# Turning one tile's keys on TensorE instead of VectorE, in a fused window-attention and feed-forward kernel

## The chip, the cores and the metric

The kernel runs on one core of a Trainium2 chip. The metric is the device time of one execution in microseconds (us). Beside it stands a profile of one execution: for each engine (TensorE or PE, its weight loads or PEld, VectorE or DVE, ScalarE or ACT, GpSimd or POOL, SyncE or SP) the instructions in order of time, what ended each wait, and the packets of the DMA queues.

## What is computed

A sliding-window causal attention (window of 64, 8 batches, 8 heads, 576 positions, head size 64), whose output is laid out as 4608 tokens of 512, goes through a gated feed-forward block:

```python
scores = scale * np.matmul(q, k.transpose(0, 1, 3, 2))
rel = pos[:, None] - pos[None, :]
mask = (rel >= 0) & (rel < window)
scores = np.where(mask, scores, -1000000000.0)
attn = softmax(scores)                      # exp, divided by the sum
x = np.matmul(attn, v)                      # then (tokens, heads * head size)
g = x @ w_gate
silu = g * (1.0 / (1.0 + np.exp(-g)))
out = silu * (x @ w_val) @ w_out            # 512 -> 1536 -> 512
```

Inputs and output are fp32; the kernel computes in bf16 with fp32 accumulation.

## The kernel before, in words

**Tiles.** The 4608 tokens are nine tiles of 512. Tile t below 7 holds the first 512 positions of batch t; tile 7 (`LAST`) gathers the last 64 positions of all batches; tile 8 is batch 7. For each tile TensorE computes scores, sums of the exponentials, the mix with the values, then twelve gate steps `m` (`gate_value`, L441: four matmuls with `w_gate` and four with `w_val`, each of 128x128 weights and 512 columns; `gate_end`: ScalarE's silu at L434, VectorE's product `hT` at L435), and later the projection with `w_out` (`project_part`, L450). Tile t's attention is run between the pieces of tile t-1's projection.

**Engines are in order.** The program is written out by hand under a manual schedule: each engine does its instructions in the order of the code. A DMA is an instruction of the engine whose queue it is put on: GpSimd issues most loads (they cast fp32 to bf16 on the way), and a copy that waits on GpSimd holds back the loads behind it.

**Memory for results.** PSUM has eight banks. Banks 0 to 3 are two tiles `two` of two banks each; banks 4 to 7 are four tiles `one`. Gate steps use banks 4 to 7 in turn, except steps 0 and 1 of tile 0, which use the `pairs` of banks (2, 3) and (0, 6).

**Tile 0** is loaded in fp32 (`raw`, `v_first`), cast (`cast_first`, L556), turned by transposes on TensorE (`turn_first`, `transposes`, L207) and copied out of PSUM by VectorE or ScalarE (`split_k`, L210, reorders the keys). Its values: the first half, `v_first`, comes fp32 over SyncE's queue and is cast into `v1` by VectorE (L633, L635); the second half comes cast over GpSimd's queue.

**Tiles 1 to 8** have their queries and keys turned by VectorE, which transposes 32x32 blocks (`turn_q`, L219, and `turn_k`, L229). For that the second 32 of the 64 head dimensions must lie in other partitions than the first. From tile 2 on the load itself arranges this (`load_q`, `load_k`, four DMAs for each part, L91 and L138). For tile 1 it is done in two steps: `load_plain` (L112, L118) brings both halves together, eight key loads and four query loads on GpSimd's queue, and `second_halves` (L130) copies the second half across partitions, one copy on GpSimd and one on ScalarE for each of keys and queries and each half of the heads (`lo`, `hi`).

**The order on GpSimd's queue in the first 50 us** is: two casts for tile 0, half of its values, ten loads of `w_gate` and `w_val` up to column 1024, tile 1's keys `lo`, weights to 1280, queries `lo`, the copy of the keys `lo`, weights to 1536, keys `hi`, the copy of the queries `lo`, `w_out` rows of chunks 0 and 1 (L199), queries `hi`, the copy of the keys `hi`, the rest of `w_out`, three loads of tile 1's values (L164), the copy of the queries `hi`, five more; then all of tile 2.

**Tile 1's turns** lie in tile 0's gate steps: keys after steps 6, 7, 10 and 11, queries after 8 and 9 and, for `hi`, behind step 11. Then come `scores(1, 0)` (L281), sixteen projection matmuls of tile 0 over four banks (`columns(0, 4)`), `scores(1, 1)`, twelve more, the sums (L314), twelve, the mix (L381), and eight. **Tile 2's turns** (`turn`, a query and a key turn for each head pair) lie behind steps 4, 6, 8 and 10 of tile 1's gates; later tiles' behind 1, 4, 7 and 10.

Of the kernel before, what the change touches and what calls it, by code (L numbers as in the profile page):

```python
# [8 lines left out]
P = 128  # L9
FP32 = mybir.dt.float32  # L10
BF16 = mybir.dt.bfloat16
# [6 lines left out]
def kernel(  # L18
# [10 lines left out]
    nc = tc.nc  # L29
    S, D, H = 576, 64, 8  # L30
# [7 lines left out]
    stage = ctx.enter_context(tc.tile_pool(name="stage", bufs=2))  # L38
# [7 lines left out]
    bank = [two[i][:, j] for i in range(2) for j in range(2)]  # L46
# [5 lines left out]
    kT = [cst.tile([P, 4, 512], BF16, name=f"kT{i}") for i in range(3)]  # L52
    v12 = cst.tile([P, 2, 4, H, D], BF16, name="v12")
    v1 = v12[:, 0]
# [3 lines left out]
    identb = cst.tile([P, P], BF16, name="identb")  # L58
# [6 lines left out]
    def batch(t):  # L65
        return t if t < LAST else t - 1
# [7 lines left out]
    staged, queries, weights, inverse, xT, hT = {}, {}, {}, {}, {}, {}  # L74

    def load_runs(eng, dst, src, t, hs):
        eng.dma_start(  # L77
            dst.rearrange("r h e d -> r h (e d)"),
            src[batch(t), hs, 0:512].rearrange("h (r e) d -> r h (e d)", e=4),
        )  # L80
# [21 lines left out]
                    )  # L102
        return q_s

    def load_plain(t, which, us):

        q_s, k_s = staged[t]
        for a in range(2):
            hs = slice(a + 2 * us.start, a + 2 * us.stop - 1, 2)
            r = slice(64 * a, 64 * a + 32)  # L110
            if which == "q":
                nc.gpsimd.dma_start(  # L112
                    q_s[r, us],
                    q[batch(t), hs, 0:512].rearrange("u (r e) d -> r u (e d)", e=16),
                )
            else:
                for u in range(us.start, us.stop):
                    nc.gpsimd.dma_start(  # L118
                        k_s[r, :, u],
                        k[batch(t), 2 * u + a, 0:512].rearrange("(g r e) d -> r g (e d)", g=4, e=4),  # L120
                    )

    def second_halves(t, which, us, a, copy):

        src, dst = slice(64 * a, 64 * a + 32), slice(64 * a + 32, 64 * a + 64)
        if which == "q":
            ap = staged[t][0][:, us].rearrange("r u (e d) -> r (u e) d", d=D)
        else:
            ap = staged[t][1][:, :, us].rearrange("r g u (e d) -> r g (u e) d", d=D)
        copy(ap[dst][..., 0:32], ap[src][..., 32:64])  # L130

    def load_k(k_s, groups):

# [26 lines left out]
    def load_halves(eng, dst, t, hds=range(H)):  # L160

        for hd in hds:
            w, x, h = hd // 4, hd // 2 % 2, hd % 2
            eng.dma_start(  # L164
                dst[64 * x:64 * x + 64, :, w, h],
                v[batch(t), hd, 0:512].rearrange("(j r) d -> r j d", r=64),
            )
# [23 lines left out]
    def weights_gv(f0, f1, c0=0, c1=4):  # L191
        for src, dst in ((moe_w_gate, wg), (moe_w_val, wv)):
            nc.gpsimd.dma_start(  # L193
                dst[:, c0:c1, f0:f1],
                src[P * c0:P * c1, f0:f1].rearrange("(c r) f -> r c f", r=P),
            )

    def weights_o(c0, c1):
        nc.gpsimd.dma_start(  # L199
            wo[:, c0:c1, :],  # L200
            moe_w_out[P * c0:P * c1].rearrange("(c r) f -> r c f", r=P),
        )
# [6 lines left out]
    def split_k(dst, tp):  # L209
        nc.vector.tensor_copy(  # L210
            dst.rearrange("p (r e) -> p r e", e=4),
            tp.rearrange("p (e r) -> p r e", e=4),
        )

    def turn_q(t, u):

        if u == 0:
            queries[t] = att.tile([P, 4, 512], BF16, name="qT", tag="qT")
        nc.vector.transpose(  # L219
            queries[t][:, u, :].rearrange("r (e x) -> r e x", e=16),  # L220
            staged[t][0][:, u].rearrange("r (e d) -> r e d", d=D)[:, :, 0:32],
        )
# [5 lines left out]
    def turn_k(dst, k_s, u):  # L228
        nc.vector.transpose(  # L229
            dst[:, u, :].rearrange("r (g x e) -> r g e x", g=4, e=4),  # L230
            k_s[:, :, u].rearrange("r g (e d) -> r g e d", d=D)[:, :, :, 0:32],
        )
# [28 lines left out]
    def half(x):  # L261
        return slice(64 * x, 64 * x + 64)
# [215 lines left out]
    def out_tile():  # L478
        return bank[4 + take("g")]
# [27 lines left out]
    v_first = stage.tile([P, 4, H, D], FP32, name="v_f", tag="v", bufs=1)  # L507
    for u in range(4):
        hs = slice(2 * u, 2 * u + 2)
# [43 lines left out]
    on_v, on_p, on_a = nc.vector.tensor_copy, nc.gpsimd.tensor_copy, nc.scalar.copy  # L553

    def cast_first(copy, u, i):
        copy(  # L556
            first[:, i, u].rearrange("r e (h d) -> r h e d", h=2),
            raw[i][:, 2 * u:2 * u + 2],
        )
# [8 lines left out]
    def weigh_first(u):  # L568
        E = eb[u][:, 1:17].rearrange("r (h y) z -> r h (y z)", h=2)
        nc.scalar.activation(E, two[u % 2][:], AF.Exp, scale=0.125)  # L570
        weights[0, u] = E
# [17 lines left out]
    cast_first(on_a, 2, 0)  # L589
    cast_first(on_p, 3, 0)  # L590
    weights_gv(0, 256, 0, 2)
    weights_gv(0, 256, 2, 4)
    weights_gv(256, 512)
    weights_gv(512, 768)
    weights_gv(768, 1024)
    q_s = stage.tile([P, 4, 16 * D], BF16, name="q_s", tag="q")
    k_s = stage.tile([P, 4, 4, 4 * D], BF16, name="k_s", tag="k")
    staged[1] = q_s, k_s
    lo, hi = slice(0, 2), slice(2, 4)
    load_plain(1, "k", lo)  # L600
    weights_gv(1024, 1280)
    load_plain(1, "q", lo)
    second_halves(1, "k", lo, 1, on_p)
    weights_gv(1280, 1536)
    load_plain(1, "k", hi)
    second_halves(1, "q", lo, 1, on_p)
    weights_o(0, 2)
    load_plain(1, "q", hi)
    second_halves(1, "k", hi, 1, on_p)
    weights_o(2, 4)  # L610
    weights_o(4, 8)
    weights_o(8, 12)
    load_halves(nc.gpsimd, vb[1], 1, range(3))
    second_halves(1, "q", hi, 1, on_p)
    load_halves(nc.gpsimd, vb[1], 1, range(3, H))

    cast_first(on_v, 2, 1)
# [12 lines left out]
    scores_first(2)  # L630
    log1()
    weigh_first(2)
    on_v(v1[:, 0], v_first[:, 0])  # L633
    turn_first(3, (4, 5))
    on_v(v1[:, 1], v_first[:, 1])  # L635
    bias_first(3)
    scores_first(3)
    weigh_first(3)
# [13 lines left out]
    log3()  # L652
    inv3()
    part_first((3,), (5,), 0, odd)
    pairs = [(bank[2], bank[3]), (bank[0], bank[6])]
    scale(0, 0, bank[0])
    scale(0, 1, bank[1])
    gate_part(0, (0, 1), pairs, 0)
# [9 lines left out]
    for m in range(12):  # L668
        if m < 2:
            gate_end(0, m, pairs[m])  # L670
        else:
            gate_value(0, m)
        if m == 2:
            for x in range(2):
                for c in range(2):
                    nc.vector.tensor_copy(
                        mask[half(x), 0, c],
                        tri[half(x), x ^ c].rearrange("r (y e) -> r e y", e=16),
                    )
            for i in (1, 2, 4):  # L680
                nc.vector.tensor_copy(mask[:, i:2 * i], mask[:, 0:i])
            for E in eb:
                nc.vector.memset(E[:, 0], 0.0)
        if m in (5, 7, 9):
            which, us = {5: ("k", lo), 7: ("q", lo), 9: ("k", hi)}[m]
            second_halves(1, which, us, 0, on_a)
        if m in (6, 7, 10, 11):
            turn_k(kT[1], staged[1][1], {6: 0, 7: 1, 10: 2, 11: 3}[m])
        if m in (8, 9):
            turn_q(1, m - 8)  # L690

    set_exp()
    second_halves(1, "q", hi, 0, on_a)
    for u in (2, 3):
        turn_q(1, u)
    tiles = [out_tile(), d_tile(), out_tile(), d_tile()]
# [18 lines left out]
    for t in range(1, NT):  # L715
        if t > 1:
            set_exp()
            scores(t, 0)
            project(t - 1, 0)
            if t == 2:  # L720
                stage_v(3)
            o_ps = out_tile()
            project_part(t - 1, (1,), (o_ps,), range(5))
            scores(t, 1)
            sums(t, 0)
            project_part(t - 1, (1,), (o_ps,), range(5, 12))
            project_end(t - 1, 1, o_ps)
            project(t - 1, 2)
            sums(t, 1)
            mix_all(t)  # L730
            project(t - 1, 3)
        set_silu()
        if t + 1 == LAST:
            load_last_v()
        elif t + 1 < NT and t > 1:
            cast_v(t + 1)
        if t + 2 < NT:
            load_qk(t + 2)
            if t > 1 and t + 2 != LAST:
                stage_v(t + 2)  # L740
        if t == 2:
            k_l = load_k(
                cast.tile([P, 4, 4, 4 * D], BF16, name="k_l", tag="c0"),
                [(b, S - P) for b in range(4, 8)],
            )
        turns = (4, 6, 8, 10) if t == 1 else (1, 4, 7, 10)
        for m in range(12):
            gate_value(t, m)
            if m in turns and t + 1 < NT:
                turn(t + 1, turns.index(m))  # L750
            if m == 8 and 3 <= t < 7:
                turn_k(kT[2], k_l, t - 3)
# [32 lines left out]
```

## Time and profile before

| what | us |
|---|---|
| median of 3 runs | 327.34 (327.29 to 328.5) |
| the profiled execution | 328.81 |
| its span, first to last instruction | 327.1 |
| TensorE busy | 315.2 |
| VectorE busy | 219.8 |
| ScalarE busy | 168.9 |
| GpSimd busy, DMA issues counted | 152.0 |
| granted TensorE clock, mean | 0.999 |

Two further rows of the profile matter for reading what follows. The page's slices show the share of busy time of an engine in 40 equal parts of the span, 8.2 us each, in tenths:

```profile
PE   7899889979999999999999999999999999999996
...
DMA  7999899999979999979940999799501300021003
```

TensorE is below nine tenths in the first slices, in the sixth (41 to 49 us) and the ninth (65 to 74 us). The chain of work that ended last, followed back from the end, is TensorE from 68 us on, apart from one passage through ScalarE near 143 us; before that it is mostly loads on GpSimd's queue.

A timeline line gives start, length, engine, line, what it writes and reads with the shapes, and in brackets the idle time before it with what ended it. Matmuls are pipelined, so each one's own length overlaps the next; the distance between starts is the cost of one in a stream.

### The profile page before, as it was taken

How to read it: one execution, taken by the hardware profiler on the slowest of the kernel's cores; microseconds unless marked ns; L12 is line 12 of the kernel's file. 1: busy time of each engine (PE TensorE's matmuls, PEld its weight loads, DVE VectorE, ACT ScalarE, POOL GpSimd, SP SyncE). 2: the span in 40 equal slices, each digit the busy share in tenths (PEclk: the TensorE clock that was granted, in tenths of full speed). 3: DMA queues.
4: the chain of work that ended last, by engine and by line, in shares of the span. 5: the costliest groups of instructions: out<-in, count | busy, mean ns of one | idle time of the engine just before them, and what ended most of it. 6: DMA issues, size and time to landing. Idle time of an engine off the chain costs nothing.

```text
span 327.1 us, 6971 instructions
## 1 busy us (share of the span) xinstructions
PE 315.2 (96%) x2708; PEld 150.4 (46%) x2750; DVE 219.8 (67%) x345; ACT 168.9 (52%) x240; POOL 152.0 (46%) x269
## 2 busy tenths in 40 slices
PE   7899889979999999999999999999999999999996
PEld 4544434434444444445444544445445544444443
DVE  4666665397857776787668766976787666774322
ACT  5855847326833583357535653475337633683310
POOL 5958765896276569556523999464110000000000
PEclk9999999999999999999999999999999999999999
DMA  7999899999979999979940999799501300021003
GB/s 253 200 195 173 127 175 180 193 106 158 184 145 204 154 161 151 199 80 179 224 94 12 145 193 101 48 176 199 124 3 28 89 16 2 2 87 43 2 16 113
DMA packets 83618, 40.36 MB, mean 123 GB/s; under 512 B 64256, under 2 KB 78848, under 8 KB 83584
## 3 DMA queue, kind: packets, MB, share of 16 engines
q0 software_dynamic: 51584, 22.59, 58.4%
q1 hardware_dynamic: 31456, 16.79, 20.9%
q10 hardware_dynamic: 544, 0.52, 0.5%
q8 instruction: 21, 0.34, 0.5%
q14 instruction: 13, 0.11, 0.1%
HBM read 53.02 MB, written 9.44 MB: 191 GB/s over the span
## 4 chain that ended last, share of the span: by engine, by line
PE 77%; DMA 15%; POOL 4%; issue 2%; ACT 1%; DVE 1%; SPq 1%; POOLq 0%; DVEq 0%
PE one L441 46%; PE one L450 24%; DMA k_s<-in_k_dram 6%; DMA wo<-in_moe_w_out_dram 3%; DMA q_s<-in_q_dram 3%; PE two L281 2%; DMA wv<-in_moe_w_val_dram 2%; PE two L381 2%; DMA q_f<-in_q_dram 2%; PE one L314 1%; POOL wg L193 1%; PE one L492 1%; POOL wv L193 1%; POOL k_s L130 1%; SPq L77 1%
## 5 line engine op out<-in xcount | busy, mean ns | idle before, releaser
L434 ACT ACTIVATE sg<-one 128x512 f32<-128x512 f32 x106 | 63.3, 597 | 111.5 <-PE one L441 88.8
L435 DVE TENSOR_TENSOR hT<-sg,one 128x512 bf16<-128x512 f32 x107 | 74.1, 693 | 57.0 <-PE one L441 54.9
L441 PE MATMUL one<-xT,wg 128*128 128x512 bf16 x416 | 108.4, 379 | 0.8
L441 PE MATMUL one<-xT,wv 128*128 128x512 bf16 x414 | 107.0, 379 | 1.9 <-DVE hT L435 1.8
L450 PE MATMUL one<-wo,hT 128*128 128x512 bf16 x397 | 93.9, 380 | 2.8 <-DMA wo<-in_moe_w_out_dram 1.0
L138 POOL DMA_DIRECT2D k_s<-in_k_dram x112 | 60.5, 552 | 27.0 <-DMA q_s<-in_q_dram 18.2
L441 PEld LDWEIGHTS <-wv 128*128 128x128 bf16 x424 | 41.5, 98 | 52.0 <-issue 2.1
L441 PEld LDWEIGHTS <-wg 128*128 128x128 bf16 x424 | 41.5, 98 | 50.2 <-issue 0.3
L450 PEld LDWEIGHTS <-hT 128*128 128x128 bf16 x420 | 39.1, 98 | 48.3 <-issue 3.7
L229 DVE STREAM_TRANSPOSE kT<-k_s 128x512 bf16<-128x512 bf16 x32 | 41.3, 1290 | 2.8 <-DMA k_s<-in_k_dram 2.8
L294 ACT ACTIVATE eb<-two 128x960 bf16<-128x960 f32 (+1 forms) x32 | 29.5, 974 | 16.8 <-PE two L281 16.7
L297 DVE TENSOR_TENSOR eb<-eb,mask 128x960 bf16<-128x960 bf16 (+1 forms) x32 | 21.4, 667 | 12.1 <-ACT eb L294 12.1
L397 DVE TENSOR_TENSOR xT<-two,r 128x512 bf16<-128x512 f32 x34 | 21.7, 686 | 6.4 <-PE two L381 4.8
L189 POOL CAST vb<-v_f 128x512 bf16<-128x512 f32 x20 | 11.4, 616 | 31.3 <-PE one L441 11.6
L219 DVE STREAM_TRANSPOSE qT<-q_s 128x512 bf16<-128x512 bf16 x32 | 22.4, 702 | 1.7 <-POOL q_s L130 1.7
L331 ACT ACTIVATE r<-r 128x512 f32<-128x512 f32 (+1 forms) x34 | 22.3, 655 | 1.0
L328 ACT ACTIVATE r<-one 128x512 f32<-128x512 f32 x32 | 18.9, 590 | 4.8 <-PE one L314 4.7
L91 POOL DMA_DIRECT2D q_s<-in_q_dram x24 | 13.0, 565 | 5.1 <-DVE qT L219 4.8
L302 DVE TENSOR_TENSOR both<-eb 128x512 bf16<-128x512 bf16 x32 | 13.6, 425 | 1.1
L500 ACT ACT_TABLE_LOAD x9 | 11.5, 1283 | 2.0 <-issue 1.9
L164 POOL DMA_DIRECT2D vb<-in_v_dram x16 | 11.0, 734 | 2.6 <-DMA wo<-in_moe_w_out_dram 2.6
L503 ACT ACT_TABLE_LOAD x9 | 11.5, 1283 | 0.2
(115 smaller groups left out, 193.4 us busy)
## 6 DMA issues: line engine op xcount, KB each, us to landing
k_s<-in_k_dram POOLq DMA_DIRECT2D x112, 56.0 KB, 5.2
q_s<-in_q_dram POOLq DMA_DIRECT2D x24, 248.0 KB, 5.4
v_f<-in_v_dram SPq DMA_DIRECT2D x40, 128.0 KB
wg<-in_moe_w_gate_dram POOLq DMA_DIRECT2D x5, 256.0 KB, 6.5
wv<-in_moe_w_val_dram POOLq DMA_DIRECT2D x5, 256.0 KB, 7.2
q_f<-in_q_dram SPq DMA_DIRECT2D x4, 256.0 KB
wo<-in_moe_w_out_dram POOLq DMA_DIRECT2D x2, 512.0 KB, 7.1
vb<-in_v_dram POOLq DMA_DIRECT2D x16, 64.0 KB, 4.2
```

Of the source, the lines that this page charges most:

```text
L138: nc.gpsimd.dma_start(k_s[p0:p0 + 32, g, :, 0:w], k[b, a:H:2, s:s + P].rearrange("u (r e) d -> r u (e d)", e=4) [:, :, 32 * c:32 * c + w],)
L219: nc.vector.transpose(queries[t][:, u, :].rearrange("r (e x) -> r e x", e=16), staged[t][0][:, u].rearrange("r (e d) -> r e d", d=D)[:, :, ...
L229: nc.vector.transpose(dst[:, u, :].rearrange("r (g x e) -> r g e x", g=4, e=4), k_s[:, :, u].rearrange("r g (e d) -> r g e d", d=D)[:, :, ...
L294: nc.scalar.activation(flat, s_ps[h][:].rearrange("r a b -> r (a b)")[:, 0:n], AF.Exp, scale=0.125)
L297: nc.vector.tensor_mul(flat, flat, mask[:].rearrange("r j c e y -> r (j c e y)")[:, 0:n])
L328: nc.scalar.activation(r, d_ps, AF.Ln)
L331: nc.scalar.activation(r, r, AF.Exp, scale=-1.0)
L397: nc.vector.tensor_mul(x, o_ps, r)
L434: nc.scalar.activation(sg[:], g_ps[:], AF.Silu)
L435: nc.vector.tensor_mul(hT[t][:, m, :], sg[:], v_ps[:])
L441: nc.tensor.matmul(ps[:], w[:, c, P * m:P * m + P], xT[t][:, c, :], start=(c == 0), stop=(c == 3),)
L450: nc.tensor.matmul(o_ps[:], hT[t][:, c, P * s:P * s + P], wo[:, c, :], start=(c == 0), stop=(c == 11),)
```

## The change

Tile 1's keys are loaded as they lie, positions in partitions, by two loads of four heads each (`raw_k`, as tile 0's `load_runs` does but cast on the way), and not copied across partitions. After gate steps 6 and 8 TensorE transposes them, for each of two head pairs eight times 128x64 into 64x128 (four position phases, two heads) into bank `u` of 0 to 3, and VectorE copies each bank out with `split_k`, as for tile 0. The eight key loads, the four key copies and VectorE's four key turns of tile 1 are gone.

GpSimd's copies of query halves stand later in its order, behind more loads; ScalarE's copy of the `lo` queries moves from step 7 to 8, and its copy of the `hi` queries goes to VectorE. Tile 1's query turns `lo` move from steps 8 and 9 to 9 and 10. The two casts of `v_first` go from VectorE to GpSimd, between its second and third weight load. The banks of `pairs[1]` are swapped: gate in bank 6, value in bank 0. Tile 2's turns move from steps 4, 6, 8, 10 to 6, 8, 10, 11.

```diff
-    def load_plain(t, which, us):
-
-        q_s, k_s = staged[t]
+    def load_plain(t, us):
+
         for a in range(2):
...
+            nc.gpsimd.dma_start(
+                staged[t][0][64 * a:64 * a + 32, us],
+                q[batch(t), a + 2 * us.start:2 * us.stop:2, 0:512]
+                .rearrange("u (r e) d -> r u (e d)", e=16),
+            )
...
     weights_gv(0, 256, 0, 2)
+    on_p(v1[:, 0], v_first[:, 0])
+    on_p(v1[:, 1], v_first[:, 1])
     weights_gv(0, 256, 2, 4)
...
-    k_s = stage.tile([P, 4, 4, 4 * D], BF16, name="k_s", tag="k")
-    staged[1] = q_s, k_s
+    raw_k = stage.tile([P, H, 4, D], BF16, name="k_r", tag="k")
+    staged[1] = q_s, None
     lo, hi = slice(0, 2), slice(2, 4)
-    load_plain(1, "k", lo)
+    load_runs(nc.gpsimd, raw_k[:, 0:4], k, 1, slice(0, 4))
     weights_gv(1024, 1280)
-    load_plain(1, "q", lo)
-    second_halves(1, "k", lo, 1, on_p)
+    load_runs(nc.gpsimd, raw_k[:, 4:8], k, 1, slice(4, 8))
+    load_plain(1, lo)
     weights_gv(1280, 1536)
-    load_plain(1, "k", hi)
-    second_halves(1, "q", lo, 1, on_p)
     weights_o(0, 2)
-    load_plain(1, "q", hi)
-    second_halves(1, "k", hi, 1, on_p)
+    second_halves(1, lo, 1, on_p)
+    load_plain(1, hi)
     weights_o(2, 4)
     weights_o(4, 8)
     weights_o(8, 12)
     load_halves(nc.gpsimd, vb[1], 1, range(3))
-    second_halves(1, "q", hi, 1, on_p)
+    second_halves(1, hi, 1, on_p)
     load_halves(nc.gpsimd, vb[1], 1, range(3, H))
...
-    on_v(v1[:, 0], v_first[:, 0])
     turn_first(3, (4, 5))
-    on_v(v1[:, 1], v_first[:, 1])
...
-    pairs = [(bank[2], bank[3]), (bank[0], bank[6])]
+    pairs = [(bank[2], bank[3]), (bank[6], bank[0])]
...
-        if m in (5, 7, 9):
-            which, us = {5: ("k", lo), 7: ("q", lo), 9: ("k", hi)}[m]
-            second_halves(1, which, us, 0, on_a)
-        if m in (6, 7, 10, 11):
-            turn_k(kT[1], staged[1][1], {6: 0, 7: 1, 10: 2, 11: 3}[m])
-        if m in (8, 9):
-            turn_q(1, m - 8)
+        if m == 8:
+            second_halves(1, lo, 0, on_a)
+        if m in (6, 8):
+            for u in (m - 6, m - 5):
+                tp = bank[u].bitcast(BF16)[:, 0:512]
+                for e in range(4):
+                    for h in range(2):
+                        nc.tensor.transpose(
+                            tp[half(h), P * e:P * e + P], raw_k[:, 2 * u + h, e], identb[:]
+                        )
+                split_k(kT[1][:, u, :], tp)
+        if m in (9, 10):
+            turn_q(1, m - 9)
 
     set_exp()
-    second_halves(1, "q", hi, 0, on_a)
+    second_halves(1, hi, 0, on_v)
...
-        turns = (4, 6, 8, 10) if t == 1 else (1, 4, 7, 10)
+        turns = (6, 8, 10, 11) if t == 1 else (1, 4, 7, 10)
```

## The prediction

> **What bounds the kernel now.** I read the page's first part, then TensorE's waits, then the timelines of TensorE, VectorE and GpSimd up to 80 us. TensorE is busy 96% of the span, so the time is its work plus its waits.
>
> ```profile
> PE 315.2 (96%) x2708; PEld 150.4 (46%) x2750; DVE 219.8 (67%) x345; ACT 168.9 (52%) x240; POOL 152.0 (46%) x269
> ```
>
> Its waits in total (us, times, longest), without the first 16 us:
>
> ```profile
> PE one L441 <- DVE hT L435: 1.8, 1, 1.8
> ...
> PE one L450 <- DMA wo<-in_moe_w_out_dram: 1.0, 2, 0.5
> ...
> PE one L450 <- DVE hT L435: 0.4, 1, 0.4
> PE two L281 <- DVE qT L219: 0.4, 1, 0.4
> ```
>
> They lie in two places: the stretch where tile 0 is projected while tile 1's scores run (37 to 53 us), and one step of tile 1's gates. In TensorE's timeline (start, length, line, last the idle time and its releaser):
>
> ```profile
> 11.12 0.62 PE L207 MATMUL one<-identb,qk_b 128*128 128x128 bf16 x8
> ...
> 13.81 0.46 PE L360 MATMUL two<-eb,v 128*64 128x64 bf16 x16
> ...
> 16.25 0.38 PE L421 MATMUL two<-xT,wg 128*128 128x512 bf16 x1 [0.22 <-DVE xT L397]
> ...
> 37.07 0.62 PE L281 MATMUL two<-qT,kT 64*64 64x128 bf16 x32
> 37.62 0.82 PE L450 MATMUL one<-wo,hT 128*128 128x512 bf16 x3
> 38.85 1.24 PE L450 MATMUL one<-wo,hT 128*128 128x512 bf16 x5 [0.41 <-DVE hT L435]
> 40.58 1.89 PE L450 MATMUL one<-wo,hT 128*128 128x512 bf16 x8 [0.49 <-DMA wo<-in_moe_w_out_dram]
> ...
> 68.05 1.02 PE L441 MATMUL one<-xT,wv 128*128 128x512 bf16 x4 [1.83 <-DVE hT L435]
> ```
>
> Four 512-column matmuls start 0.864 us after the four before them, so one costs 0.216 us; a gate step (one m) is eight, 1.73 us. VectorE in the same time:
>
> ```profile
> 11.90 0.68 DVE L210 COPY kT<-one 128x512 bf16<-128x512 bf16 x1
> ...
> 14.90 1.29 DVE L397 TENSOR_TENSOR xT<-two,r 128x512 bf16<-128x512 f32 x2 [0.64 <-PE one L360]
> ...
> 28.61 0.69 DVE L435 TENSOR_TENSOR hT<-sg,one 128x512 bf16<-128x512 f32 x1 [1.04 <-PE one L441]
> 29.22 1.32 DVE L229 STREAM_TRANSPOSE kT<-k_s 128x512 bf16<-128x512 bf16 x1
> ...
> 66.16 1.32 DVE L229 STREAM_TRANSPOSE kT<-k_s 128x512 bf16<-128x512 bf16 x1 [2.83 <-DMA k_s<-in_k_dram]
> ```
>
> At 66.16 VectorE has stood 2.83 us for tile 2's keys; the hT behind it is late and TensorE stands. GpSimd, which issues the loads, does the same to itself earlier: it waits for keys before a copy, and the wo loads stand behind.
>
> ```profile
> 35.41 1.03 POOL L130 COPY k_s<-k_s 32x1024 bf16<-32x1024 bf16 x1 [1.84 <-DMA k_s<-in_k_dram]
> 36.39 2.22 POOL L199 DMA_DIRECT2D wo<-in_moe_w_out_dram x3
> ```
>
> The windows view has 196 GB/s from 13 to 27 us, but 110 GB/s from 37 to 42.
>
> **The change, part by part**, on the profiled clock.
>
> *Swap of the second gate pair's banks.* At 16.25 a matmul into bank[0] waits for VectorE. bank[0]'s own reader, the first of the two xT products begun at 14.90, is done at 15.5; the second, which reads bank[1], ends at 14.90 + 1.29 = 16.19. So both halves of a tile `two` are guarded as one. With bank[6] first, that matmul goes ahead: -0.17 (0 to -0.22).
>
> *Two casts of v1 on GpSimd* (0.61 to 0.88 us each by its own L556 casts) stand between its second and third weight load at 10.6 us: the loads behind are issued 1.2 to 1.8 later. The values were issued by SyncE at 4.5 and 4.9 and their packets end by 10.8, so no wait. The cover is the queue: values and first weights are in it until about 13.7. The tightest load is wv 256:512, issued at 12.71 and landed at 19.19 in the chain, read at 20.57: 1.2 us of slack after the swap. I take 0; if nothing is hidden, up to +0.6. VectorE gains nothing: qT at 11.56 follows the end of its transposes anyhow.
>
> *Keys by two loads.* The same bytes. An issue on GpSimd follows the landing of the load eight places earlier (the chain: a load issued at 12.71 lands at 19.19, the eighth after it goes out at 19.47); two loads for eight leave more bytes in flight, and no key copy stops GpSimd. The first four heads landed at 26.00; now about 26.4, needed by TensorE at 28.2. The second load, about two weight loads of 1.35 and its own 1.3 later, at 30.4, is needed at 33.5. Both hidden; beyond those margins each us late is one lost. The query copy that GpSimd still waits for (q landed about 31.5) now has wo 0:2 and the last weights issued ahead of it. Those weights landed at 33.9 against 34.4 before; the later gates only widen that. No cost.
>
> *Transposes on TensorE.* 32, in groups of eight: two after m=6, two after m=8. Price: sixteen 128*64 matmuls of 64 columns in 0.28 us (13.81 to 14.09), that is 17.5 ns as the two column halves overlap; for 128 columns 35 ns, 0.28 a group. Upper bound: eight full transposes at 11.12 start 0.56 before what follows them. I take 0.28, nearest in shape. But the second group of each pair writes the other half of the tile `two` that VectorE's copy of the first group (split_k) reads, and by the finding at 16.25 it must wait for that copy. The changed program has that wait: the ninth transpose waits for VectorE's count after the first split_k. In VectorE's order split_k stands behind hT of the same step. By before's rows: m=6 ends at 28.34, first group 28.62; hT 28.61 to 29.22; split_k 0.68, to 29.90; second group 29.96 (L210 to TensorE took 0.06 at 12.64) to 30.24. So m=7 starts 1.90 late. Twice: +3.80 (unpaired 0.56: first group still behind hT, +4.36; VectorE 0.1 quicker each time: +3.6). The loss is TensorE's: m=7 and all behind it wait.
>
> By the Trainium skill ("TensorE: Matmul & The Clock Gate", Part 4: PE-mode transpose) a transpose in a kernel takes some 275 ns and does not count as work that holds the full clock. The trace disagrees: 69 ns each at a granted clock of 1.00 between 5 and 15 us. By the page, as an estimate, each pair would cost 5.1 instead of 1.9 and the kernel would end 6.5 us later than below.
>
> *The projection stretch.* Before, 36.97 (end of m=11) to 53.12 (tile 1's first gate), 16.15 us. Its matmuls, at their own steps: scores 0.55, 16 columns 3.46, scores 0.55, 12 columns 2.59, and from the sums at 46.88 on 6.24 as before: 13.39. The 2.76 between goes, because its causes do: two key turns of 1.29 no longer stand ahead of m=11's hT (steps 9 and 10 hold one 0.7 query turn each, 11 none); wo lands earlier, and TensorE comes 3.6 later; GpSimd's second query copy ends near 39.3 (before 41.7), VectorE's new copy (0.6 from L302's 0.42 for half as many; at most 1.1, as on ACT and GpSimd) and two turns run from 41.5 to 43.5, against 44.6 when scores need them. ACT loses a 1.04 copy ahead of the exponentials. Taken -2.76; if the waits on queries and hT keep half, -2.1; at best -3.0.
>
> *Tile 2's turns at m = 6, 8, 10, 11.* The first key turn falls at about 67.4, its keys landed at 65.9 before and are now issued some 4 us earlier: the stall (68.05 against 66.06) goes, -1.99. New: turns after 10 and 11 in a row. Before, tile 2's masks began at 78.07 on VectorE, its sums' second half needed them at 80.85 and had them at 80.2. A fourth turn (1.73 from 74.97 to 76.70) behind m=11's hT at 77.33 puts the masks at 79.06, 0.99 later, ready at 81.2: +0.41 (0.2 to 0.7).
>
> Sum: -0.17 + 3.80 - 2.76 - 1.99 + 0.41 = **-0.7**. The profiled execution took 328.81, a span of 327.1 and 1.7 around it; the median of three is 327.34. I put the difference on the median: **326.6**.
>
> **Rivals.** *The waits go and the pairs don't stall*: if TensorE ran both groups through, 2 x 1.34 less: -3.4, 323.9. For it: the groups write different banks. Against it: 16.25 and the wait in the program. *Weights late*: GpSimd's casts sit at the head of the one queue that feeds everything. Past 1.2 us of delay in the stream each us stalls m=2; past 3.6 the kernel is slower by over 0.5%. At 4 us: +2.8, 329.4. It takes casts that wait for the values until 13 us, or are slowed to 2 us; for it, one cast took 0.88 instead of 0.61 beside VectorE; against it, packets over by 10.8 and a queue still full. *The keys turn late does nothing*: were the 66 us stall to stay, with the rest as above, +1.3, 328.6; against it, VectorE only asks 1.5 us after the old landing.
>
> **How the numbers follow.** Forecast 0.66, pairs without stall 0.14, weights late 0.10, stall stays 0.05, the rest beyond these. The ends of the terms give -1.4 to +1.6 with all at one side; the range takes a little beyond the first and most of the second: 325.4 to 328.3. A measurement tells about 0.5% (1.6 us) from no change: faster 0.16, same 0.70, slower 0.14.
>
> **What would show it.** Right: two idle gaps of about 1.3 us on TensorE inside the k transposes after m=6 and m=8, released by the copy into kT; no wait for wo, hT or qT between 40 and 54; no gap near 66; 0.4 before tile 2's first sums. Wrong: no such gaps, transposes far from 35 ns, a wait for wv near 20 or for keys at 28 or 33, or hT late in the projection.

## The result, and the profile after

The changed kernel took 330.38 us (median of 12 runs, 329.55 to 331.33), beside 327.6 us (327.1 to 329.37) for the kernel before in the same series: a ratio of 1.008, with a 95% interval of 1.0062 to 1.0097. It is slower by 2.8 us, where 0.7 us less was forecast, and lies outside the range of 325.4 to 328.3. The profiled execution took 330.95, a span of 329.2, against 328.81 and 327.1 before: +2.1 from one span to the other.

The page's first part and slices for the changed kernel:

```profile
PE 318.4 (97%) x2739; PEld 151.8 (46%) x2782; DVE 217.8 (66%) x344; ACT 165.8 (50%) x237; POOL 148.4 (45%) x263
...
PE   7998899999999999999999999999999999999995
...
DMA  7999999999589999969950999899601300021013
```

TensorE's dips at the sixth and ninth slice (41 to 49 and 65 to 74 us) are filled, and its 31 further instructions are the transposes, less one record. The fourth slice (25 to 33 us) is now at eight tenths where it was at nine, and the fifth stays at eight; the two pairs of transposes lie there. Busy time and its share rose, and the kernel is slower: the waits and the starts say more than the sum. TensorE's waits from 16 us on, in total, times and longest:

```profile
PE two L677 <- DVE kT L198: 2.2, 2, 1.1
PE one L438 <- issue: 0.3, 2, 0.2
PE two L409 <- DVE xT L385: 0.3, 1, 0.3
PE one L302 <- DVE both L290: 0.2, 1, 0.2
```

Gone are the waits for `hT` (1.8 and 0.4), for `w_out` (1.0) and for `qT` (0.4). In their place stand two waits of 1.1 for the copy into `kT`, at the transposes (L677). In TensorE's timeline:

```profile
5.17 1.04 PE L195 MATMUL one<-identb,qk_b 128*128 128x128 bf16 x8 [0.63 <-ACT qk_b L544]
...
7.70 1.04 PE L195 MATMUL one<-identb,qk_b 128*128 128x128 bf16 x8
8.66 0.64 PE L227 MATMUL two<-bias,identb 64*64 64x512 bf16 x4
...
17.13 0.38 PE L409 MATMUL two<-xT,wg 128*128 128x512 bf16 x1 [0.27 <-DVE xT L385]
...
28.79 1.03 PE L429 MATMUL one<-xT,wv 128*128 128x512 bf16 x4
29.75 0.41 PE L677 MATMUL two<-identb,k_r 128*64 128x128 bf16 x8
31.27 0.41 PE L677 MATMUL two<-identb,k_r 128*64 128x128 bf16 x8 [1.10 <-DVE kT L198]
31.61 1.04 PE L429 MATMUL one<-xT,wg 128*128 128x512 bf16 x4
...
35.17 0.41 PE L677 MATMUL two<-identb,k_r 128*64 128x128 bf16 x8
36.69 0.41 PE L677 MATMUL two<-identb,k_r 128*64 128x128 bf16 x8 [1.10 <-DVE kT L198]
...
49.67 1.02 PE L302 MATMUL two<-both,ones 64*64 64x512 bf16 x8
50.62 2.76 PE L438 MATMUL one<-wo,hT 128*128 128x512 bf16 x12
...
56.21 1.02 PE L429 MATMUL one<-xT,wg 128*128 128x512 bf16 x4
...
82.35 0.40 PE L302 MATMUL one<-both,ones 64*64 64x512 bf16 x2 [0.17 <-DVE both L290]
```

Without the transposes, step 7 would have begun 0.864 after 28.79, at 29.65. It begins at 31.61, 1.96 later. (The first three lines are read in the last section.) VectorE shows what the second group waited for:

```profile
29.93 0.69 DVE L423 TENSOR_TENSOR hT<-sg,one 128x512 bf16<-128x512 f32 x1 [1.04 <-PE one L429]
30.53 0.68 DVE L198 COPY kT<-two 128x512 bf16<-128x512 bf16 x1
31.72 0.69 DVE L198 COPY kT<-two 128x512 bf16<-128x512 bf16 x1 [0.51 <-PE two L677]
```

The copy of the first group stands behind step 6's `hT` and ends at 31.21; the second group starts at 31.27.

To see where time went, I cut the span at five starts on TensorE: gate step 2 of tile 0, the first scores of tile 1, the first gate of tile 1, the first scores of tile 2, the first gate of tile 2. Each column is the time from the mark before (the first from the span's start, the last to the span's end). "Again" is the same kernel profiled a second time, in the runs below.

| us | to step 2 | step 2 to 11, tile 0 | projection | tile 1's gates | to tile 2's gate | rest | span |
|---|---|---|---|---|---|---|---|
| before | 19.71 | 17.36 | 16.05 | 22.80 | 13.08 | 238.12 | 327.1 |
| before, again | 19.65 | 17.36 | 16.09 | 22.67 | 13.08 | 238.21 | 327.1 |
| after | 21.02 | 21.30 | 13.89 | 20.81 | 13.66 | 238.56 | 329.2 |
| after, again | 20.11 | 21.74 | 13.89 | 20.81 | 13.66 | 238.57 | 328.8 |

The four middle parts behave as forecast, within 0.6. What the forecast lacked is at the two ends: the head, +1.31 in one profile and +0.40 in the other where -0.17 was forecast, and the rest, +0.44.

### The profile page after: what moved, and what is told of

Its sections match the earlier page's. It is cut to its first block, busy times and chain, and to the rows that moved or that the text cites. A ratio compares the mean times of both kernels' runs of the same rounds, so it can differ in the third digit from the quotient of the medians.

```text
span 329.2 us, 7015 instructions
## 1 busy us (share of the span) xinstructions
PE 318.4 (97%) x2739; PEld 151.8 (46%) x2782; DVE 217.8 (66%) x344; ACT 165.8 (50%) x237; POOL 148.4 (45%) x263
## 4 chain that ended last, share of the span: by engine, by line
PE 93%; DVE 4%; issue 1%; DMA 1%; ACT 0%; DVEq 0%
PE one L429 55%; PE one L438 27%; PE two L269 2%; PE two L369 2%; PE one L302 1%; DMA q_f<-in_q_dram 1%; DVE hT L423 1%; PE one L195 1%; PE two L409 1%; PE one L480 1%; DVE kT L198 1%; PE two L240 0%; DVE kT L217 0%; DVE qT L207 0%; PE two L227 0%
## 5 line engine op out<-in xcount | busy, mean ns | idle before, releaser
L217 DVE STREAM_TRANSPOSE kT<-k_s 128x512 bf16<-128x512 bf16 x28 | 36.1, 1288 | 0.0
L91 POOL DMA_DIRECT2D q_s<-in_q_dram x24 | 13.0, 556 | 4.7 <-DVE qT L207 4.7
L98 POOL DMA_DIRECT2D q_s<-in_q_dram x16 | 8.6, 627 | 7.0 <-DVE qT L207 7.0
```

The lines of the kernel that those rows point to most:

```text
L217: nc.vector.transpose(dst[:, u, :].rearrange("r (g x e) -> r g e x", g=4, e=4), k_s[:, :, u].rearrange("r g (e d) -> r g e d", d=D)[:, :, ...
```

## The experiments

The theory after the result was: the pair wait costs what was forecast, and the surplus is the two casts on GpSimd, which delay the loads behind them. The rivals: the late turns of tile 2 are the surplus; it belongs to the executions that happened to be measured; or the removed stalls were worth less than their size in one profile. Every ratio below is to the kernel before in the same series on the same chip; series differ in chip, so medians are compared only inside one series.

### The kernel before, and the changed kernel, once more

No edit.

> The kernel before, unchanged, profiled once more. Theory 1: half speed of TensorE's first matmuls is a matter of the single execution (in the two profiles the full clock is granted from 5.7 us before the change and from 10.1 after it, and the loads that TensorE waits for landed 0.35 us later in the second, ahead of every changed instruction); then this profile can show either, and the first gate step of the loop begins near 19.7 us or near 21.2. Theory 2: the late clock belongs to the change; then every profile of the kernel before grants it by 6 us, and the times of this one lie within 0.3 us of before.

> The changed kernel once more, on the chip of the other runs. Sums of its stages in the profiles against before, from the first loop gate on: +3.94 (transposes), -2.16 (projection), -1.93 (tile 1's gates), +0.58 (tile 2's sums), +0.43 (end) = +0.9. Theory 1: the rest of the measured +2.8 is that the two profiled executions of before, at 328.8, were slower than its median of 327.6 to 328.2; then this lies 1.5 to 2.5 above before here too, and its profile from the first loop gate on is as the first one within 0.2 us. Theory 2: the rest is a late clock in each execution of this kernel: the profile grants the full clock near 10 us again.

Before: 328.51 against 328.18, ratio 1.001 (0.9989 to 1.0031). Changed: 330.49 against 328.4, ratio 1.0055 (1.0034 to 1.0076), +2.1 us. The first series gave +2.8 with an interval of 2.0 to 3.2 us, so both agree on some 2 to 2.5 us of loss, and its sign isn't an accident of one execution. The waits of the repeated changed kernel from 16 us on:

```profile
PE two L677 <- DVE kT L198: 2.2, 2, 1.1
PE one L429 <- DMA wg<-in_moe_w_gate_dram: 0.4, 1, 0.4
...
PE one L429 <- DMA wv<-in_moe_w_val_dram: 0.3, 1, 0.3
```

In its timeline the two waits for weights stand at gate step 2, the first to read columns 256 to 512, which are loaded behind the casts:

```profile
15.66 0.38 PE L409 MATMUL two<-xT,wg 128*128 128x512 bf16 x1 [0.27 <-DVE xT L385]
...
20.11 1.04 PE L429 MATMUL one<-xT,wg 128*128 128x512 bf16 x4 [0.40 <-DMA wg<-in_moe_w_gate_dram]
21.41 0.82 PE L429 MATMUL one<-xT,wv 128*128 128x512 bf16 x3 [0.26 <-DMA wv<-in_moe_w_val_dram]
```

The idle time in brackets counts from the end of the matmul before, whose length would have overlapped the next; by the starts the two waits cost more. From the first matmul on `xT` to step 2 it is 4.45 (15.66 to 20.11) instead of 3.89 in the first profile (17.13 to 21.02), and the second half of step 2 starts 1.30 after the first instead of 0.864: 0.56 and 0.44, together 1.00. In the first profile TensorE reached step 2 only at 21.02, and the weights were there.

### The pair wait taken out

```diff
-                tp = bank[u].bitcast(BF16)[:, 0:512]
+                tp = bank[(0, 2, 1, 3)[u]].bitcast(BF16)[:, 0:512]
```

The two groups of a pair now write different tiles `two`.

> The changed kernel with the transposes of head pairs 0, 1, 2, 3 into banks 0, 2, 1, 3, so that two groups in a row lie in different tiles of two banks and the second need not wait for the copy of the first. Theory 1 (the wait costs what the profile shows): no gap in the transposes after steps 6 and 8, and 2 x 1.1 to 1.35 = 2.2 to 2.7 us faster than the changed kernel, about 327.9. Theory 2 (VectorE only moves the wait, as its two copies and hT of one step take 1.9 us against a step of 1.73): under 1 us faster.

Measured 328.03 against 328.18, ratio 0.9995 (0.9977 to 1.0013): clear of the changed kernel's 1.0055 and 1.008. In its timeline:

```profile
28.40 0.64 PE L677 MATMUL two<-identb,k_r 128*64 128x128 bf16 x16
28.97 1.04 PE L429 MATMUL one<-xT,wg 128*128 128x512 bf16 x4
...
32.53 0.64 PE L677 MATMUL two<-identb,k_r 128*64 128x128 bf16 x16
33.10 1.04 PE L429 MATMUL one<-xT,wg 128*128 128x512 bf16 x4
```

Sixteen transposes run through in 0.57, without a gap. This settles both halves of the transposes' term: the price of one (0.57 / 16 = 36 ns) and the guard of a tile of two banks as a whole. The 2.2 of gaps are gone, and at 43.86 a wait of 0.76 for `w_out` has come in, since TensorE is there earlier.

### Tile 2's turns back, casts back, each alone

```diff
-        turns = (6, 8, 10, 11) if t == 1 else (1, 4, 7, 10)
+        turns = (4, 6, 8, 10) if t == 1 else (1, 4, 7, 10)
```

> The changed kernel with tile 2's turns back behind steps 4, 6, 8 and 10. Theory 1: the late turns were needed only as long as tile 2's keys landed late; in the changed kernel's profile they landed by 66.8 us and step 4 of tile 1 is at 64, so the stall comes back in part: 0 to 2 us against the 0.6 us before tile 2's sums that goes: -0.6 to +1.4 us to the changed kernel. Theory 2: the keys are early enough: 0.6 us faster, no gap.

Measured 329.63 against 328.18, ratio 1.005 (1.0033 to 1.0068); the changed kernel's was 1.0055, so the medians don't tell them apart. The stages do: from tile 2's scores to its first gate 13.08 instead of 13.66, and tile 1's gates 20.81 as with the late turns, that is, no stall at step 4. The late turns removed nothing in the changed kernel, because its keys come earlier anyway, and cost 0.58.

```diff
     weights_gv(0, 256, 0, 2)
-    on_p(v1[:, 0], v_first[:, 0])
-    on_p(v1[:, 1], v_first[:, 1])
     weights_gv(0, 256, 2, 4)
...
+    on_v(v1[:, 0], v_first[:, 0])
     turn_first(3, (4, 5))
+    on_v(v1[:, 1], v_first[:, 1])
```

> The changed kernel with the two casts of the first values back on VectorE. Theory 1: the casts on GpSimd cost nothing on the path: within 0.3 us of the changed kernel (330.4). Theory 2: they cost the first 20 us something (clock or late weights): 1 to 1.5 us faster than the changed kernel.

Measured 329.89 against 328.18, ratio 1.0055 (1.0034 to 1.0076): no difference that can be measured from the changed kernel. Its profile reaches step 2 at 19.44 without a wait for a weight (20.11 in the repeated profile with the casts on GpSimd), but its second pair wait is 1.50 instead of 1.10. Taken by itself the median speaks against the theory. The pair waits make it a weak test, though: they delay TensorE by 3.9 just behind the stretch in which late loads would be felt. So the casts had to be tried where nothing covers them.

### One part alone, in the kernel before

Two edits of the change were put into the kernel before, each in a kernel of its own.

```diff
-        turns = (4, 6, 8, 10) if t == 1 else (1, 4, 7, 10)
+        turns = (6, 8, 10, 11) if t == 1 else (1, 4, 7, 10)
```

> The kernel before with nothing but tile 2's turns behind steps 6, 8, 10 and 11. By the profiles the stall of 1.9 us at 66 us goes and 0.6 us before tile 2's sums comes: -1.3 us. Theory 1 (that stall is in every execution): 1.0 to 1.5 us faster than before. Theory 2 (it waits for loads whose time varies, and was long in the two profiled executions): 0 to 0.8 us faster, with a gap in this profile as predicted all the same.

Measured 327.7 against 328.4, ratio 0.9989 (0.9965 to 1.0012): -0.7, and no difference can be excluded. By its stages tile 1's gates took 20.81 (the stall is gone, -1.99 to -1.86 against the two profiles of before), but 0.58 came in before tile 2's sums and 0.5 in the projection of tile 0 (16.57 against 16.05), where this execution waited 1.31 in one piece for `w_out`. The stall is real, and one profile says what it was in that execution only: tile 1's gates take 22.80 and 22.67 in two profiles of the kernel before, and 21.57 and 21.72 in the two kernels that follow here, which have tile 2's turns as before.

```diff
     weights_gv(0, 256, 0, 2)
+    on_p(v1[:, 0], v_first[:, 0])
+    on_p(v1[:, 1], v_first[:, 1])
     weights_gv(0, 256, 2, 4)
...
-    on_v(v1[:, 0], v_first[:, 0])
     turn_first(3, (4, 5))
-    on_v(v1[:, 1], v_first[:, 1])
```

> The kernel before with nothing but the two casts of the first values moved from VectorE to GpSimd, between its second and third weight load. Theory 1 (the loads behind them come 1.7 to 2 us later, and their lead is not enough): waits for wv or wg at 20 to 24 us or more of the waits for wo and tile 2's keys; 0.5 to 1.6 us slower than before. Theory 2 (the forecast's: the queue is full until the late loads arrive): within 0.3 us of before.

Measured 329.96 against 328.1, ratio 1.0061 (1.0034 to 1.0088): +1.9 us, from two casts that were costed at nothing (its profiled span is 328.2 against 327.1). TensorE's waits from 16 us on:

```profile
PE one L450 <- DMA wo<-in_moe_w_out_dram: 2.7, 3, 1.4
PE one L441 <- DVE hT L435: 0.6, 1, 0.6
...
PE one L441 <- DMA wv<-in_moe_w_val_dram: 0.3, 1, 0.3
PE one L441 <- DMA wg<-in_moe_w_gate_dram: 0.2, 1, 0.2
```

Against the kernel before, the wait for `w_out` went from 1.0 (0.6 in its second profile) to 2.7 and the weights of step 2 are late; the stall for tile 2's keys is smaller in this execution, 0.6 instead of 1.8. GpSimd's timeline in the changed kernel shows how it begins; the kernel with the casts alone has the same gap, 0.59:

```profile
10.03 0.71 POOL L181 DMA_DIRECT2D wv<-in_moe_w_val_dram  x1
10.81 0.61 POOL L580 CAST v<-v_f 128x512 bf16<-128x512 f32 x1
11.98 0.62 POOL L581 CAST v<-v_f 128x512 bf16<-128x512 f32 x1 [0.57 <-DMA v_f<-in_v_dram]
12.54 0.70 POOL L181 DMA_DIRECT2D wg<-in_moe_w_gate_dram  x1
```

The third weight load goes out at 12.54 instead of 10.58, that is 2.51 after the second instead of 0.70, a stop of 1.8: two casts, and between them a wait for the second half of `v_first`. The last packet on SyncE's queue, which brings it, ended at 11.16 in the changed kernel and at 10.77 with the casts alone, and the second cast started 0.8 after it in both. To part the stop from the wait, one cast was moved alone:

```diff
     weights_gv(0, 256, 0, 2)
+    on_p(v1[:, 0], v_first[:, 0])
     weights_gv(0, 256, 2, 4)
...
-    on_v(v1[:, 0], v_first[:, 0])
     turn_first(3, (4, 5))
```

> The kernel before with one of the two casts, that of the values that land first, on GpSimd between its second and third weight load: the issue stands 0.6 us, without a wait for a landing, where two casts and that wait held it 1.8 us. With both, the queue moved 98 to 158 GB/s from 13 to 20 us instead of 182 to 198 and the loads landed 1.5 to 2.4 us later. Theory 1 (the queue has to run dry first: two loads of 128 KB bridge 0.6 us): the rate stays near 190 from 13 us on, landings later by at most 0.3, time within 0.4 us of before. Theory 2 (each stop of the issue is paid in full or more): landings 0.6 to 1 later, 0.5 to 1 us slower.

Measured 328.36 against 328.22, ratio 1.0014 (0.999 to 1.0038): a stop of 0.6 costs nothing that can be measured, the upper end of the interval being 1.2. The windows view (stretch, length, busy time of TensorE, its weight loads, VectorE, ScalarE and GpSimd, granted clock, mean busy time of a DMA engine, GB/s) for the kernel before, then with two casts alone, then with one:

```profile
13.00:16.00 3.00, 2.73 (x93) 2.05 (x91) 1.26 (x4) 2.86 (x5) 3.00 (x5) 1.00 1.45 195
16.00:19.00 3.00, 2.78 (x19) 1.27 (x18) 1.48 (x3) 2.19 (x3) 2.10 (x4) 1.00 1.45 196
```

```profile
13.00:16.00 3.00, 2.73 (x101) 2.04 (x91) 1.17 (x3) 2.79 (x5) 3.00 (x5) 1.00 1.16 137
16.00:19.00 3.00, 2.78 (x19) 1.28 (x19) 1.56 (x3) 2.27 (x3) 3.00 (x5) 1.00 1.05 124
```

```profile
13.00:16.00 3.00, 2.73 (x105) 2.07 (x98) 1.53 (x4) 2.66 (x5) 3.00 (x5) 1.00 1.43 188
16.00:19.00 3.00, 3.00 (x19) 1.27 (x18) 1.68 (x3) 2.40 (x4) 2.57 (x5) 1.00 1.29 164
```

Last number: 195 and 196 GB/s before, 137 and 124 with two casts, 188 and 164 with one. The loss isn't only the 1.8 us of the stop. For six us behind it the queue moves two thirds of what it did, and the weights for columns 256 to 512 of `w_val` land at 21.38 instead of 19.19. GpSimd is busy all of 13 to 16 us in all three, with five issues each, so the number of issues in that stretch doesn't explain the rate. What holds it down that long is open; it wasn't tried by itself.

### Putting the parts together

```diff
-                tp = bank[u].bitcast(BF16)[:, 0:512]
+                tp = bank[(0, 2, 1, 3)[u]].bitcast(BF16)[:, 0:512]
...
-        turns = (6, 8, 10, 11) if t == 1 else (1, 4, 7, 10)
+        turns = (4, 6, 8, 10) if t == 1 else (1, 4, 7, 10)
```

> The changed kernel with the transposes' banks in the order 0, 2, 1, 3 and tile 2's turns back at steps 4, 6, 8, 10. Theory 1: the two gains add: 0.6 us below the kernel with the banks alone (328.0), 327.4, with no gap in tile 1's gates. Theory 2: without the pair waits TensorE comes 2.1 us earlier to step 4 and tile 2's keys are late again: 327.5 to 329, a gap near 62 us.

This is the changed kernel with both the pairs' banks and tile 2's turns mended: 328.77 against 328.4, ratio 1.0009 (0.9986 to 1.0032). It missed what was expected: the time lies in theory 2's range, but the gap near 62 isn't there (20.81 for tile 1's gates in the table below), and it is no better than the mended pairs alone. With it the casts were tested again, moved back to VectorE with the same edit as above, this time with no pair wait to cover them:

> As the kernel with banks and turns, and the two casts of values back on VectorE as well. Theory 1 (GpSimd's casts hold back the stream of weights by the 1.5 us that they take and wait, and it shows where TensorE is no longer late: 0.28 for wv at 20 us and 0.76 for wo at 43 in the kernel with the banks alone): another 0.7 to 1.1 us, about 326.5 and faster than before. Theory 2 (the stream is bound by the queue's own rate): within 0.3 us of the kernel with banks and turns.

Measured 327.15 in the same series, ratio 0.996 (0.9941 to 0.9979). The intervals don't meet: the casts cost 1.6 here. Where, these two profiles don't show: the one with the casts on GpSimd has a late clock (last section) and no wait for a weight, and its execution is one of the fastest of its twelve. So by the medians their price depends on what else TensorE waits for: +1.9 in the kernel before, nothing that can be told in the changed kernel, 1.6 once the pair waits are gone.

The two last kernels are this one with tile 2's turns at steps 5, 7, 8 and 10, and the same with one more matmul in the run of dummy matmuls at the start (`keep_warm(6)` to `keep_warm(7)`).

```diff
-        turns = (4, 6, 8, 10) if t == 1 else (1, 4, 7, 10)
+        turns = (5, 7, 8, 10) if t == 1 else (1, 4, 7, 10)
...
-    keep_warm(6)
+    keep_warm(7)
```

The first hunk alone:

> The kernel with banks, turns and casts mended, with tile 2's turns behind steps 5, 7, 8 and 10 instead of 4, 6, 8 and 10. The profile there showed a wait of 1.2 us for tile 2's keys on VectorE, 0.4 of it passed on to TensorE. Theory 1: a step later the keys are there: 0.2 to 0.4 us faster (326.8), no gap in tile 1's gates. Theory 2: two turns in a row at 7 and 8 put hT behind by as much: no change.

Both:

> As the kernel with turns 5, 7, 8, 10, with seven instead of six 512-column matmuls that keep TensorE busy until the first data. In ten profiles the full clock is granted at 10.1 and 10.4 us where TensorE stood 0.6 us before the first transposes, and at 4.4 to 6.4 where it stood 0.2 to 0.4. Theory 1 (that gap decides it): the gap is under 0.3, the clock comes before 6.5, the slow executions go and the median falls 0.2 to 0.6 us. Theory 2 (chance alone): the median is the same or 0.2 us slower.

Measured 326.7 and 326.46 against 328.1: ratios 0.9962 (0.994 to 0.9984) and 0.9954 (0.9939 to 0.9969). Both beat the kernel before and the changed one. The 0.24 between them can't be told from chance. The spans of the single executions say a little more: without the additional matmul nine of twelve took 324.3 to 325.0 and three 325.9 to 326.3; with it all twelve took 324.3 to 325.0. That is what theory 1 expects, and three in twelve are too few to call it shown. The stages of the kernels that matter here:

| us | to step 2 | step 2 to 11, tile 0 | projection | tile 1's gates | to tile 2's gate | rest | span |
|---|---|---|---|---|---|---|---|
| pair wait out | 19.22 | 19.16 | 14.31 | 20.81 | 13.66 | 238.56 | 325.7 |
| turns back | 19.78 | 21.30 | 13.89 | 20.81 | 13.08 | 238.57 | 327.4 |
| casts alone | 20.12 | 18.01 | 17.34 | 21.57 | 13.08 | 238.12 | 328.2 |
| pairs and turns | 21.01 | 18.71 | 13.89 | 20.81 | 13.08 | 238.57 | 326.1 |
| all three | 19.58 | 18.71 | 13.89 | 21.20 | 13.08 | 238.57 | 325.0 |
| and turns between, bridge | 19.24 | 18.71 | 13.90 | 20.81 | 13.08 | 238.57 | 324.3 |

## Why the prediction was wrong, step by step

The forecast of -0.7 stood on six terms. Four held within 0.6 us; that of the turns held in the profile only; the casts were costed at nothing and cost 1.9 by themselves. They are the largest single part of the miss that the profiles show, 1.00 of 2.37 in the changed kernel's repeated profile, and not the whole of it. The end of the kernel was left out.

*Swap of the banks, -0.17: right.* In TensorE's timeline the first matmuls on `xT` up to the short one that follows them take 0.95 (17.13 to 18.08) instead of 1.12 (15.65 to 16.77), and the wait of 0.22 at the fourth of them is gone. The whole head grew all the same, for other reasons.

*Two casts on GpSimd, 0: this is the step that failed.* It rested on two sentences. "Their packets end by 10.8, so no wait": GpSimd waited 0.57 for the second half of `v_first`, until 11.98; a waiting engine went on 0.8 after the last packet. "The cover is the queue", with values and first weights in it until about 13.7: between 13 and 16 us it moved 137 instead of 195 GB/s in the kernel with the casts alone. The bound of +0.6 counted the delay of the issue at one load. The runs show +1.9: the queue moves less for six us, the load of that bound is issued 1.6 later (14.28 instead of 12.71) and lands 2.2 later (21.38 instead of 19.19), and with the casts alone the larger wait comes at `w_out`, which the bound left out. The rival "weights late" named the place and the point from which it decides, 1.2 us of delay with step 2 stalled: a landing 2.2 later makes 1.0 by its rule, and 1.00 is what the starts of the repeated profile show. It priced 4 us of delay at 329.4, though; that the median of 330.38 lies near there is not its doing alone. Its chance of 0.10 was too small, since all that spoke against it were the two sentences above.

*Keys by two loads, no cost: right.* No transpose waits for `k_r` in the profiles of the changed kernel or of those derived from it.

*Transposes, +3.80: measured +3.94.* The gap was 1.10 instead of 1.34 long, and the transposes with what stands around them took 0.86 a pair instead of 0.56. The row of the trace was the right one: sixteen transposes in 0.57. The 275 ns that the prediction took from the Trainium skill are the length of one transpose; the profile has such a length too, 223 ns on average for these 32, and what one costs in a stream is the distance between starts, 36 ns here. So page and trace don't contradict each other there, and the 6.5 us worked out from a length were no estimate of this cost.

*Projection stretch, -2.76: measured -2.16.* From the end of step 11, as the prediction counted, 13.99 (42.22 to 56.21) instead of 13.39. All four waits went, but the sums now take 0.95 (49.67 to 50.62) where they took 0.65 in the kernel before, as they come before the last of `both` (VectorE writes it from 49.81 to 50.23), and 0.3 is spread over the joints. The lower bound of the term, -2.1, holds it. The sums in the kernel before:

```profile
46.88 0.71 PE L314 MATMUL two<-both,ones 64*64 64x512 bf16 x8
47.53 2.76 PE L450 MATMUL one<-wo,hT 128*128 128x512 bf16 x12
```

*Tile 2's turns, -1.99 and +0.41: measured -1.99 and +0.58, in the profile.* The first is a difference between two executions. The kernels with both casts or one of them moved, which have the same turns, had a stall about 1.1 smaller in their profiles, and the late turns alone moved the median by 0.7 only. And in the changed kernel the turns weren't what removed it: with the old steps back, there was no stall either. So the late turns were a pure loss of 0.58 there.

*What was not in the sum:* the rest of the kernel from tile 2's first gate on, 238.56 instead of 238.12 in every kernel derived from the changed one. All of it lies behind the last output: the DMA that writes it is issued 235.1 after the first gate of tile 2 in both kernels, and the span ends 3.43 after that issue instead of 3.00 (3.44 in the second profile of the changed kernel, 3.00 in that of the kernel with the casts alone). In that stretch SyncE waits for TensorE's sequencer, 1.1 in all in the nine profiles of kernels with the changed keys and 0.7 in the five without. Why it waits longer is open.

Added up on the repeated profile, with the forecast's -0.7: head +0.57 (0.40 instead of -0.17), step 2 to 11 +0.58 (4.38 instead of 3.80), projection +0.60, turns +0.17, rest +0.45. The weights behind the casts are 0.56 of the first and 0.44 of the second. That is 2.37 more, or +1.7 in the span; the medians gave +2.1 and +2.8. In the first profile the head stands 1.48 above its forecast instead, with a late clock (last section) and no wait for a weight. The remaining 0.4 to 1.1 between this span and the medians isn't assigned to a part.

## What to carry to other kernels

An instruction put between loads on an issuing queue is costed by what the queue is doing behind it, not by its own length: look at the rate of the microseconds that follow, at the tightest consumer and at the later ones, and take a wait for a landing as a wait until it is shown not to be one. Before writing a new group of results, look at which buffer tile the group before it left to be copied out: if two banks are one tile, alternate tiles. A stall in one profile is worth its length in that execution only, and when two edits remove the same stall, one of them is paid for nothing.

## What the runs showed of the hardware

**The start of the full clock varies, and can cost more than the edit under study.** In twelve profiles the trace has the clock granted in full from between 4.4 and 7.1 us; in two, the first one of the changed kernel and that of the kernel with pairs and turns mended, from 10.1 and 10.4. Those two reach gate step 2 at 21.0, the others at 19.2 to 20.1. In both, TensorE had stood 0.63 and 0.58 before the first transposes; in the rest 0.24 to 0.48, or nothing. The kernel before has, in its timeline,

```profile
4.82 1.04 PE L207 MATMUL one<-identb,qk_b 128*128 128x128 bf16 x8 [0.28 <-ACT qk_b L556]
...
6.98 0.62 PE L207 MATMUL one<-identb,qk_b 128*128 128x128 bf16 x8
7.53 0.41 PE L239 MATMUL two<-bias,identb 64*64 64x512 bf16 x4
```

Eight transposes at 6.98 took 0.55 here, and the eight at 7.70 in the changed kernel 0.96, before its clock was full. With one more dummy matmul the gap was closed:

```profile
3.48 1.48 PE L509 MATMUL one<-ones 128*64 128x512 bf16 x3
4.93 0.62 PE L195 MATMUL one<-identb,qk_b 128*128 128x128 bf16 x8
```

There the clock was full from 4.8 us. The Trainium skill ("TensorE: Matmul & The Clock Gate", Part 1: what's actually happening) describes windows of about 3.4 us that run freely, one of which has to be busy before the clock goes up, so that the start varies from run to run. The clock records of the 14 traces show a window of that length: the full clock lasts 317.44, 320.85 or 324.27 us in each, which is 93, 94 or 95 times 3.413. One such step before 10.1 and 10.4 lie 6.7 and 7.0, among the starts of the other twelve, so the two late executions are late by one window. The stretches of 3.413 us that end there hold their gaps of 0.63 and 0.58; with one cast the clock was full at 6.1 although the same stretch before it held a gap of 0.48. This fits a gap that decides somewhere between 0.48 and 0.58, and two late executions don't prove it. Both late kernels have the two casts on GpSimd, as four of the others do; the gaps end by 5.2 and the casts start at 10.4 or later, so nothing here ties one to the other.

**A queue of loads that was stopped doesn't come back at once.** A stop of 0.6 us cost nothing measurable (188 and 164 GB/s in the two stretches from 13 to 19 us, against 195 and 196), and one of 1.8 us lowered the rate there to 137 and 124 GB/s.
